# Products of constants on TensorE in the last steps of a decode attention and behind the first piece of its output matrix

## The chip, the cores and the metric

The kernel runs on one core of one Trainium2 chip. The metric is the device time of one execution in microseconds; the time before is the median of three runs. The profile is one further execution, recorded by the hardware profiler.

## The reference

One decode step of a block: a layer norm, attention over a window of a cache with an output matrix, and a gated feed-forward branch whose SiLU multiplies the attention's result.

```python
def _A_ref(x, k_cache, v_cache, wq, wo):
    B, Sq, D = x.shape
    Hq, Dh = 32, 128
    Hkv, Sk = k_cache.shape[1], k_cache.shape[2]
    W = min(4096, max(256, Sk // 4))
    rep = Hq // Hkv
    q = (x @ wq).reshape(B, Sq, Hq, Dh)   # heads to the front
    k = jnp.repeat(k_cache[:, :, Sk - W:, :], rep, axis=1)
    v = jnp.repeat(v_cache[:, :, Sk - W:, :], rep, axis=1)
    scores = jnp.einsum("bhqd,bhkd->bhqk", q, k) * (Dh ** -0.5)
    p = _softmax(scores, axis=-1)
    o = jnp.einsum("bhqk,bhkd->bhqd", p, v)
    return o.reshape(B, Sq, Hq * Dh) @ wo   # heads back in place

def _B_ref(x, w_gate, w_up, w_down):
    return (_gelu(x @ w_gate) * (x @ w_up)) @ w_down

x = A_x
xn = _layernorm(x, axis=-1)
s = _A_ref(xn, A_k_cache, A_v_cache, A_wq, A_wo)
g = _silu(_B_ref(xn, B_w_gate, B_w_up, B_w_down))
return x + s * g
```

There are 8 batch rows, one query position, D = 512, 32 query heads on 8 key heads of width 128, a cache of 4096 positions of which the last 1024 count, and F = 1792. All inputs are bf16. K and V of the window are 16 MiB each, wq and wo 4 MiB each, the feed-forward weights 5.25 MiB: some 47.6 MB are read once.

## The kernel before, in words

**Transfers.** Everything large comes through one queue, SP's, into a pool `big` of nine buffers, in this order: wq, gate and up weights, then K and V of the key heads in turn (with the down weights among them), and last wo. `load_wo` (L125) fetches wo in seven pieces, listed in `pieces` (L639): heads 0 to 3 whole (2 MB), heads 4 and 5 (1 MB), then heads 6 and 7 in halves, and the last half of head 7 in two quarters.

**Sets and steps.** The attention is cut into 16 sets, two for each key head; a set has four batch rows, whose 1024 positions lie on 32 partitions each. The loop at L578 runs 44 steps, t = 0 to 43; two steps belong to a set, and `s, i = divmod(t, 2)`. The order of instructions on every engine is the order in which the program issues them (`manual_schedule`). One set passes through these stages, some steps apart:

- `transpose_quarter` (L439): TensorE turns K into PSUM tiles `kT_ps`, four buffers of a pool; VectorE (L450) and ScalarE (L452) copy them out in turn. The last set is turned in step 31.
- `scores` (L461): products of the queries (in the tile `zeros`) and the turned K; VectorE (L469) adds a mask and finds maxima.
- `maxima` (L480), `exponentials` (L494, ScalarE), `turn` (L504, VectorE).
- `value_half` (L510): the two halves of the value product, eight matmuls each on four groups of 32 columns of the array, into `o_ps`, of which there is one buffer; after the second half ScalarE copies it to `blk` (L522). In step t it treats half (t - 9) % 2 of set (t - 9) // 2, as long as that set exists: sets 12 to 15 in the steps 33 to 40.
- `gather` (L526): for one key head, sums over partitions of two sets' `blk` (L532), a reciprocal (L537), a scaling (L539), a transposition (L550) into `oR` or, for the last two heads, `oL`. The last three gathers stand in steps 33, 37 and 41.

In the steps 33 to 43 there are, on TensorE, only these: a gather and the last `maxima` in step 33, the value halves in steps 33 to 40, gathers in 37 and 41; steps 42 and 43 issue nothing.

**The output matrix.** Behind the loop, `project` (L618) multiplies each piece of wo with `oR` (heads 0 to 5, L621, on four groups of 32 columns, into `s_ps`) or `oL` (heads 6 and 7, L629, into `l_ps`). Behind piece 1 VectorE copies `s_ps` to `s_sb` (L649); behind piece 2 TensorE adds that into `l_ps` (L652). At the end VectorE multiplies with the gate (L657), adds x (L658), and ScalarE's queue stores the result (L659).

`ident` is a 128 x 128 identity in bf16, made near the start. `zeros` is a tile of 1316 columns that is cleared at the start; its first 1024 columns are the queries from then on that they are written (L345, L347).

Of the kernel before, what the change touches and what calls it, by code (L numbers as in the profile page):

```python
# [12 lines left out]
FP32 = mybir.dt.float32  # L13
# [4 lines left out]
def kernel(  # L18
# [13 lines left out]
    nc = tc.nc  # L32
# [11 lines left out]
    P = nc.NUM_PARTITIONS  # L44
# [8 lines left out]
    NS = Hkv * NB  # L53
# [6 lines left out]
    QP = CP // QT  # L60
# [15 lines left out]
    ps_kT = ctx.enter_context(tc.tile_pool(name="ps_kT", bufs=4, space=PSUM))  # L76
# [64 lines left out]
    for k0, cuts in ((0, (1, 1)), (2, (2,))):  # L141
        t = big.tile([P, 2, Hq * Dh], BF16, name="big")
# [10 lines left out]
    ident = lead.tile([P, P], BF16, name="ident")  # L153
# [15 lines left out]
    zeros = rows.tile([P, sum(sizes)], BF16, name="zeros")  # L169
# [136 lines left out]
    for k in range(NDC):  # L306
        w = wq_rows[k]
        for t in range(NT):
            for g in range(NQB):
# [4 lines left out]
                    start=(k == 0), stop=(k == NDC - 1), skip_group_check=True,  # L314
# [39 lines left out]
    for w, src in enumerate((B_w_gate, B_w_up)):  # L354
        for k0 in range(0, NDC, KW):
            wt = load_rows(src, k0, KW, NDC, "gu")
            for k in range(KW):
                for g in range(NQB):
# [3 lines left out]
                        start=(k0 + k == 0), stop=(k0 + k == NDC - 1),  # L362
# [73 lines left out]
    def transpose_quarter(s, i):  # L436
        ps = ps_kT.tile([P, QP, P], FP32, name="kT_ps")
        for c in range(QP):
            nc.tensor.transpose(  # L439
                ps[:, c, :],  # L440
                K[s][:, 2 * (i * QP + c) : 2 * (i * QP + c) + 2, :]
                .rearrange("p c d -> p (c d)").bitcast(FP32),
                identf,
            )
        if i == 0:
            kT[s] = kT_pool.tile([P, CP, P, 2], BF16, name="kT")
        out = kT[s][:, i * QP : (i + 1) * QP].rearrange("p c k e -> p (c k e)")
        in_ = ps.rearrange("p c k -> p (c k)").bitcast(BF16)
        if i % 2 == 0:
            nc.vector.tensor_copy(out=out, in_=in_)  # L450
        else:
            nc.scalar.activation(out=out, in_=in_, func=ACT.Copy)  # L452
# [24 lines left out]
    def maxima(s):  # L477

        ps = m_top
        nc.tensor.matmul(  # L480
            ps, top.pop(s).to_broadcast([P, P]), identf, start=True, stop=True
        )
        scr = small.tile([P, P], FP32, name="scr", bufs=1)
        bias = small.tile([P, 1], FP32, name="bias")
        nc.vector.tensor_tensor_reduce(  # L485
            out=scr, in0=ps, in1=same.rearrange("p x n -> p (x n)"),
            op0=ALU.add, op1=ALU.min, scale=-scale, scalar=-NEG, accum_out=bias,
        )
        biases[s] = bias

    def exponentials(s):
        blk[s] = small.tile([P, 2, Dh + 1], FP32, name="blk", bufs=6)
        P_[s] = p_pool.tile([P, CP * 32], BF16, name="p")
        nc.scalar.activation(  # L494
            out=P_[s], in_=sc.pop(s), func=ACT.Exp, scale=scale, bias=biases.pop(s),
            accum_out=blk[s][:, 0, Dh : Dh + 1],
        )
        nc.gpsimd.tensor_copy(  # L498
            out=blk[s][:, 1, Dh : Dh + 1], in_=blk[s][:, 0, Dh : Dh + 1]
        )  # L500

    def turn(s):
        pT[s] = p_pool.tile([P, CP, 32], BF16, name="pT", bufs=5)
        nc.vector.transpose(  # L504
            out=pT[s].rearrange("p c k -> p (c k)"), in_=P_.pop(s)
        )
# [3 lines left out]
    def value_half(s, i):  # L510
        if i == 0:
            o_ps[s] = ps_o.tile([P, 2, Dh], FP32, name="o_ps")
        for c in range(i * CP // 2, (i + 1) * CP // 2):
            q = c % NR
            nc.tensor.matmul(  # L515
                o_ps[s][32 * q : 32 * q + 32].rearrange("p c d -> p (c d)"),
                pT[s][:, c, :],
                V[s][:, 2 * c : 2 * c + 2, :].rearrange("p c d -> p (c d)"),
                start=(c < NR), stop=(c >= CP - NR), skip_group_check=True,
            )  # L520
        if i == 1:
            nc.scalar.activation(out=blk[s][:, :, 0:Dh], in_=o_ps.pop(s), func=ACT.Copy)  # L522
            pT.pop(s)
            V.pop(s)

    def gather(h):  # L526

        ps = m_out
        for b in range(NB):
            t = blk.pop(h * NB + b)  # L530
            for c in range(2):
                nc.tensor.matmul(  # L532
                    ps, sums[:, c, b].rearrange("p j b f -> p (j b f)"), t[:, c, :],
                    start=(b == 0 and c == 0), stop=(b == NB - 1 and c == 1),
                )
        rec = small.tile([P, 1], FP32, name="rec")
        nc.vector.reciprocal(out=rec, in_=ps[:, Dh : Dh + 1])  # L537
        o = small.tile([P, rep, Dh // rep], BF16, name="o")
        nc.vector.tensor_scalar(  # L539
            out=o, in0=ps[:, 0:Dh].rearrange("p (i r) -> p r i", r=rep),  # L540
            scalar1=rec, scalar2=None, op0=ALU.mult,
        )

        if h < HM:
            out = oR[:, h].rearrange("p r b -> p (r b)")
        else:

            out = oL[:, h - HM].rearrange("p (f y) -> p f y", f=NQB)[:, :, 0:128]
            out = out.rearrange("p f (y z) -> p y f z", z=PB)[:, :, :, 0]
        nc.vector.transpose(out=out, in_=o.rearrange("p r i -> p (r i)"))  # L550


    down_tiles = []
    AHEAD = 3
# [6 lines left out]
    def fetch(kind, h):  # L561
        while True:
            k, i = pending.pop(0)
            if k == "D":
                down_tiles.append(load_rows(B_w_down, 0, NFC, NFC, "wd"))
            else:
                sets = load_pair(
                    A_k_cache if k == "K" else A_v_cache, i,
                    2 if (k, i) in (("V", Hkv - 1),) else 1,
                )  # L570
                for y in range(NB):
                    (K if k == "K" else V)[NB * i + y] = sets[y]
            if (k, i) == (kind, h):
                return
# [3 lines left out]
    for t in range(2 * NS + LV + 3):  # L578
        s, i = divmod(t, 2)
        if i == 0 and 0 <= s - 2 < NS:  # L580
            exponentials(s - 2)
        if s < NS:
            if i == 0 and s % NB == 0:
                fetch("K", s // NB)
            transpose_quarter(s, 2 * i)
        if i == 1 and s >= 6 and s % 2 == 0:
            gather((s - 6) // 2)
        if s < NS:
            transpose_quarter(s, 2 * i + 1)
        for _ in range(2):  # L590
            if hidden_steps:
                hidden_steps.pop(0)()
        if i == 0 and 0 <= s - 2 < NS:
            turn(s - 2)
        if i == 0 and 0 <= s - 1 < NS:
            scores(s - 1)
        if i == 1 and 0 <= s - 1 < NS:
            maxima(s - 1)
        if t == LV - 1:
            fetch("D", 0)  # L600
            down(0)
        if t == LV:
            down(1)
        if t == LV + 1:
            fold()
            gate()
        s3, i3 = divmod(t - LV, 2)
        if 0 <= s3 < NS:
            if i3 == 0 and s3 % NB == 0:
                fetch("V", s3 // NB)  # L610
            value_half(s3, i3)


    s_ps = ps_s.tile([P, 128], FP32, name="s")
# [3 lines left out]
    def project(h, r):  # L618
        for q in range(NQB):
            if h < HM:  # L620
                nc.tensor.matmul(  # L621
                    s_ps[32 * q : 32 * q + 32, :], oR[:, h, r, :],
                    ws[h, r][:, q * 128 : (q + 1) * 128],
                    start=(h == 0 and r == 0), stop=(h == HM - 1 and r == rep - 1),
                    skip_group_check=True,
                )
            else:
                a = q * 128 + r * 32
                nc.tensor.matmul(  # L629
                    l_ps, oL[:, h - HM, a : a + 32],  # L630
                    ws[h, r][:, q * 128 : (q + 1) * 128],
                    start=(h == HM and r == 0 and q == 0),
                    stop=(h == Hkv - 1 and r == rep - 1 and q == NQB - 1),
                    skip_group_check=True,
                )
# [6 lines left out]
    for n, (h0, r0, nr, nh) in enumerate(pieces):  # L642
        t = load_wo(h0, r0, nr, nh)
        for h in range(h0, h0 + nh):
            for r in range(r0, r0 + nr):
                ws[h, r] = t[h - h0][:, r - r0, :]
                project(h, r)
        if n == 1:
            nc.vector.tensor_copy(out=s_sb, in_=s_ps)  # L649
        if n == 2:  # L650

            nc.tensor.matmul(  # L652
                l_ps, pick, s_sb, start=False, stop=False, skip_group_check=True
            )
# [37 lines left out]
```

## Time and profile before

| | |
|---|---|
| median of three runs | 120.62 us (120.59 to 120.70) |
| the profiled execution's own time | 120.43 us |
| its span, first to last instruction | 118.7 us |
| TensorE busy | 83.3 us, 70% of the span, 976 matmuls |
| VectorE, ScalarE, GpSimd busy | 65.1, 56.2, 6.7 us |
| SP's queue | 47.45 MB, 95.3% of 16 engines' span |
| mean rate of the transfers | 401 GB/s |
| chain that ended last | DMA 73%, TensorE 10%, VectorE 8% |

The span runs from the first to the last instruction of the program; the execution's time has 1.7 us around it. A row of the timeline merges instructions that follow each other: start, duration from the first's start to the last's end, engine, line, operation, tiles, shapes, count, and in brackets how long the engine was idle before and who ended that. The ends of matmuls are modelled and overlap with the next ones' starts. In the slices each digit is a fortieth of the span, in tenths of it busy.

### The profile page before, as it was taken

The page shows a single profiled execution, that of the slowest core. Times are in us where ns is not written, and L with a number is a line of the kernel's source. Part 1 is how long each engine was busy: PE and PEld are TensorE (multiplying, and loading weights), DVE is VectorE, ACT ScalarE, POOL GpSimd, SP SyncE. Part 2 cuts the span into 40 slices and gives each one's busy share as a digit, 9 for nine tenths or more (in the row PEclk, how much of TensorE's full clock was granted, in tenths as well). Part 3 has the DMA queues.
Part 4 walks back from the last instruction along what each step waited for, and adds up shares of the span by engine and source line. Part 5 has one row for each costly group of instructions (what it writes and reads, how often), then busy time and mean ns, then how long its engine had stood idle before and what let it go on. Part 6 is the DMA issues. An engine that isn't in the chain of part 4 may idle for free.

```text
span 118.7 us, 2391 instructions
## 1 busy us (share of the span) xinstructions
PE 83.3 (70%) x976; PEld 58.6 (49%) x976; DVE 65.1 (55%) x172; ACT 56.2 (47%) x94; POOL 6.7 (6%) x29
## 2 busy tenths in 40 slices
PE   0070639519956399699999969787795988776390
PEld 0020216119743366377677547555573755555380
DVE  0410131812799899648678658485673955734301
ACT  0500030204961887838685884676565577232000
POOL 7400000000000000000000000000000000000000
PEclk9999999999999999999999999999999999999999
DMA  3999999999999999999999999999999999999950
GB/s 99 425 450 442 401 449 403 431 431 423 423 453 414 423 425 425 428 420 428 428 431 420 425 428 425 420 431 425 425 431 428 420 428 434 413 416 420 410 192 3
DMA packets 6825, 47.60 MB, mean 401 GB/s; under 512 B 536, under 2 KB 800, under 8 KB 1952
## 3 DMA queue, kind: packets, MB, share of 16 engines
q1 hardware_dynamic: 6752, 47.45, 95.3%
q8 instruction: 7, 0.11, 0.3%
q10 hardware_dynamic: 64, 0.02, 0.1%
q14 instruction: 2, 0.02, 0.0%
HBM read 47.46 MB, written 0.01 MB: 400 GB/s over the span
## 4 chain that ended last, share of the span: by engine, by line
DMA 73%; PE 10%; DVE 8%; ACT 3%; SPq 2%; issue 1%
DMA big<-in_A_k_cache_dram 47%; DMA big<-in_A_wo_dram 26%; PE kT_ps L439 6%; PE sc L629 2%; DVE h_row L387 2%; DVE sc_sb L469 1%; DVE pT L504 1%; ACT L380 1%; SPq L145 1%; DVE kT L450 1%; SPq L96 1%; ACT kT L452 1%; PE s L407 1%; ACT p L494 1%; PE sc L461 1%
## 5 line engine op out<-in xcount | busy, mean ns | idle before, releaser
L452 ACT ACTIVATE kT<-kT_ps 128x1024 bf16<-128x1024 bf16 x32 | 32.4, 1020 | 23.4 <-PE kT_ps L439 23.2
L439 PE MATMUL kT_ps<-identf,big 128*128 128x128 f32 x256 | 37.7, 292 | 6.7 <-DMA big<-in_A_k_cache_dram 6.7
L439 PEld LDWEIGHTS kT_ps<-identf,big 128*128 128x128 f32 x256 | 30.1, 149 | 14.2 <-DMA big<-in_A_k_cache_dram 8.5
L450 DVE COPY kT<-kT_ps 128x1024 bf16<-128x1024 bf16 x32 | 22.0, 688 | 15.9 <-PE kT_ps L439 15.6
L494 ACT ACTIVATE p<-sc_sb,bias 128x512 bf16<-128x512 f32 x16 | 11.5, 718 | 6.7 <-DVE bias L485 6.3
L515 PE MATMUL o_ps<-big,pT 128*32 128x256 bf16 x256 | 12.5, 274 | 2.7 <-ACT blk L522 1.5
L504 DVE STREAM_TRANSPOSE pT<-p 128x512 bf16<-128x512 bf16 x16 | 11.3, 705 | 2.6 <-ACT p L494 2.4
L480 PE MATMUL m_ps<-identf,top 128*128 128x128 f32 x32 | 7.3, 310 | 5.9 <-DVE top L469 4.1
L469 DVE CUSTOM_DVE_ANT_0 sc_sb<-sc,own 128x512 f32<-128x512 f32 x16 | 10.5, 654 | 0.0
L461 PE MATMUL sc<-kT,zeros 128*32 128x512 bf16 x128 | 10.0, 388 | 0.5 <-ACT kT L452 0.5
L515 PEld LDWEIGHTS <-pT 128*32 128x32 bf16 x256 | 5.8, 94 | 7.6 <-issue 1.9
L532 PE MATMUL m_ps<-blk,sums 128*128 128x129 f32 x64 | 9.3, 286 | 0.0
L480 PEld LDWEIGHTS m_ps<-identf,top 128*128 128x128 f32 x32 | 4.7, 187 | 8.1 <-DVE top L469 4.9
L532 PEld LDWEIGHTS m_ps<-blk,sums 128*128 128x128 f32 x64 | 8.1, 191 | 0.9 <-issue 0.2
L498 POOL COPY blk<-blk 128x1 f32<-128x1 f32 x16 | 2.9, 183 | 97.3 <-ACT p L494 97.3
L522 ACT ACTIVATE blk<-o_ps 128x256 f32<-128x256 f32 x16 | 6.1, 382 | 3.0 <-PE o_ps L515 3.0
L311 PE MATMUL sc<-big,zeros 128*32 128x512 bf16 x16 | 2.5, 612 | 4.3 <-DMA big<-in_A_wq_dram 3.9
L318 DVE CAST q_row<-sc 128x512 bf16<-128x512 f32 x2 | 1.3, 686 | 7.5 <-PE sc L311 7.5
L485 DVE CUSTOM_DVE_ANT_0 scr<-m_ps,same 128x128 f32<-128x128 f32 x16 | 4.6, 289 | 1.4 <-PE m_ps L480 1.4
L322 ACT ACTIVATE q_row<-o_ps 128x512 bf16<-128x512 f32 x2 | 1.1, 594 | 7.6 <-PE o_ps L311 7.6
L194 PE MATMUL s<-ident,xhat 8*128 8x8 bf16 x4 | 0.3, 174 | 6.2 <-DVE xhat L185 6.2
L311 PEld LDWEIGHTS <-zeros 128*32 128x32 bf16 x32 | 1.1, 120 | 6.4 <-issue 5.8
(77 smaller groups left out, 61.0 us busy)
## 6 DMA issues: line engine op xcount, KB each, us to landing
big<-in_A_k_cache_dram SPq DMA_DIRECT2D x8, 2048.0 KB, 33.0
big<-in_A_v_cache_dram SPq DMA_DIRECT2D x7, 2048.0 KB, 33.7
big<-in_A_wq_dram SPq DMA_DIRECT2D x2, 1024.0 KB, 5.7
big<-in_A_wq_dram SPq DMA_DIRECT2D x1, 2048.0 KB, 11.2
big<-in_A_v_cache_dram SPq DMA_DIRECT2D x2, 1024.0 KB, 28.9
big<-in_A_wo_dram SPq DMA_DIRECT2D x1, 2048.0 KB
big<-in_B_w_gate_dram SPq DMA_DIRECT2D x1, 1792.0 KB, 15.0
big<-in_B_w_up_dram SPq DMA_DIRECT2D x1, 1792.0 KB, 18.5
```

The costliest lines, as they stand in the source:

```text
L439: nc.tensor.transpose(ps[:, c, :], K[s][:, 2 * (i * QP + c) : 2 * (i * QP + c) + 2, :] .rearrange("p c d -> p (c d)").bitcast(FP32), identf,)
L450: nc.vector.tensor_copy(out=out, in_=in_)
L452: nc.scalar.activation(out=out, in_=in_, func=ACT.Copy)
L461: nc.tensor.matmul(ps[32 * R : 32 * R + 32], qT[:, e, s].rearrange("p c b j -> p (c b j)"), t[:, :, 32 * R : 32 * R + 32, e], start=(e == ...
L469: nc.vector.tensor_tensor_reduce(out=sc[s], in0=ps.rearrange("p c k -> p (c k)"), in1=own.rearrange("p c b g -> p (c b g)"), op0=ALU.add, ...
L480: nc.tensor.matmul(ps, top.pop(s).to_broadcast([P, P]), identf, start=True, stop=True)
L485: nc.vector.tensor_tensor_reduce(out=scr, in0=ps, in1=same.rearrange("p x n -> p (x n)"), op0=ALU.add, op1=ALU.min, scale=-scale, scalar=- ...
L494: nc.scalar.activation(out=P_[s], in_=sc.pop(s), func=ACT.Exp, scale=scale, bias=biases.pop(s), accum_out=blk[s][:, 0, Dh : Dh + 1],)
L504: nc.vector.transpose(out=pT[s].rearrange("p c k -> p (c k)"), in_=P_.pop(s))
L515: nc.tensor.matmul(o_ps[s][32 * q : 32 * q + 32].rearrange("p c d -> p (c d)"), pT[s][:, c, :], V[s][:, 2 * c : 2 * c + 2, :].rearrange("p ...
L522: nc.scalar.activation(out=blk[s][:, :, 0:Dh], in_=o_ps.pop(s), func=ACT.Copy)
L532: nc.tensor.matmul(ps, sums[:, c, b].rearrange("p j b f -> p (j b f)"), t[:, c, :], start=(b == 0 and c == 0), stop=(b == NB - 1 and c == 1),)
```

## The change

A helper `keep(n)` is added. It takes a fresh tile of the pool behind `kT_ps` and issues n matmuls into it, with the identity as the stationary operand and the first 512 columns of `zeros` as the moving one. It is called with 2 at the end of each step t of the loop with t > 32, and with 3 behind the matmuls of the first piece of the output matrix. Nothing reads the tiles.

```diff
@@ -548,6 +548,12 @@
         nc.vector.transpose(out=out, in_=o.rearrange("p r i -> p (r i)"))
+
+    def keep(n):
+
+        ps = ps_kT.tile([P, QP * P], FP32, name="kT_ps")
+        for _ in range(n):
+            nc.tensor.matmul(ps, ident, zeros[:, 0 : QP * P], start=True, stop=True)
 
 
     down_tiles = []
@@ -609,6 +615,8 @@
             if i3 == 0 and s3 % NB == 0:
                 fetch("V", s3 // NB)
             value_half(s3, i3)
+        if t > 2 * NS:
+            keep(2)
 
 
     s_ps = ps_s.tile([P, 128], FP32, name="s")
@@ -645,6 +653,8 @@
             for r in range(r0, r0 + nr):
                 ws[h, r] = t[h - h0][:, r - r0, :]
                 project(h, r)
+        if n == 0:
+            keep(3)
         if n == 1:
             nc.vector.tensor_copy(out=s_sb, in_=s_ps)
         if n == 2:
```

Here P is 128, QP is 4 and NS is 16.

## The prediction

> **What bounds the kernel now.** I read the page's slices first, then the end of the chain in order of time, then TensorE's timeline in the last 13 us.
>
> ```profile
> PE   0070639519956399699999969787795988776390
> ...
> DMA  3999999999999999999999999999999999999950
> ```
>
> The transfers run without a break from the first slice to the 38th: the span is what 47.6 MB need at about 425 GB/s, plus what is left to do once the last piece is there. The chain in order of time shows that rest (start, duration, what):
>
> ```profile
> 82.17 30.54 DMA big<-in_A_wo_dram
> 112.70 0.04 issue
> 112.75 0.63 PE s L621 x32
> 113.38 0.00 issue
> 113.38 0.61 PE sc L629 x8
> ```
>
> Until 112.70 the output matrix is being fetched. From 112.75 to 115.79 TensorE multiplies nearly without a gap, and then come two small VectorE steps and the store. So work added on TensorE before 112.75 is free only as far as it fits into TensorE's waits; all beyond that moves the end one for one. The waits are in TensorE's timeline (start, duration, instruction, in brackets the idle time before and who ended it):
>
> ```profile
> 102.98 0.62 PE L515 MATMUL o_ps<-big,pT 128*32 128x256 bf16 x16
> 104.64 0.62 PE L515 MATMUL o_ps<-big,pT 128*32 128x256 bf16 x16 [1.04 <-ACT blk L522]
> 105.19 1.27 PE L532 MATMUL m_ps<-blk,sums 128*128 128x129 f32 x8
> 106.39 0.62 PE L515 MATMUL o_ps<-big,pT 128*32 128x256 bf16 x16
> 107.50 0.62 PE L515 MATMUL o_ps<-big,pT 128*32 128x256 bf16 x16 [0.49 <-ACT blk L522]
> 108.05 1.27 PE L532 MATMUL m_ps<-blk,sums 128*128 128x129 f32 x8
> 110.30 1.08 PE L621 MATMUL s<-big,oR 128*32 128x128 bf16 x64 [0.98 <-DMA big<-in_A_wo_dram]
> 112.75 0.63 PE L621 MATMUL s<-big,oR 128*32 128x128 bf16 x32 [1.37 <-DMA big<-in_A_wo_dram]
> ...
> 114.09 1.69 PE L629 MATMUL sc<-big,oL 128*32 128x128 bf16 x24
> ```
>
> Each row of 16 is the two halves of one value product (L510). Idle is printed from the modelled end of a product, which lies up to 0.2 us behind the moment at which the next could start; I count from start to start.
>
> **The change, part by part.** It removes and moves nothing, issues no transfer, and puts 25 products of 512 columns into TensorE's stream: two at the end of each of the steps t = 33 to 43 (22), three behind piece 0 of the output matrix. Step 33 holds the first half of the value product of set 12, so the first pair stands inside the row at 102.98; pairs follow each of the eight halves up to set 15 (steps 33 to 40), and three pairs the last gather (steps 41 to 43). Nobody reads the results. Operands and buffers are ready: `ident` and `zeros` were written near the start, and the four buffers of `kT_ps` had their last reader at 98.81 + 1.02 = 99.83.
>
> Price of one product: the trace has none of 512 columns on the full 128*128 array. Nearest from above: L333, the same array with bf16, whose rows of 128 columns follow each other at (1.89 - 0.31) / 15 = 0.105 us, so 0.42 for 512. Nearest by length: L461 moves 512 columns through four 32-column groups at once, and its second round starts 0.22 behind the first:
>
> ```profile
> 99.88 0.40 PE L461 MATMUL sc<-kT,zeros 128*32 128x512 bf16 x4 [0.52 <-ACT kT L452]
> ...
> 100.10 0.40 PE L461 MATMUL sc<-kT,zeros 128*32 128x512 bf16 x4
> ```
>
> From below: if products could run four side by side as these do, 0.22 / 4 = 0.055 each. A product on all 128 columns leaves no room beside it, and L629 just behind gives the same pace ((1.69 - 0.22) / 23 = 0.06 for 128 columns with its wait, 0.056 without), so I take **0.22**. 22 of them: 4.84 us.
>
> Price of a change between the 128*32 and the 128*128 array: eight L439 at 95.89 are followed by L461 at 96.91, 1.02 later; four L439 at 92.48 are followed by L532 of their own shape at 92.97, 0.49 later. The four more cost 4 x 0.109 = 0.44, so the change of shape costs 1.02 - 0.49 - 0.44 = 0.09. L515 to L439 (95.56 to 95.89, two rounds of 0.11) gives 0.11; I take 0.095. Before the matrix the pairs add eight changes behind the halves and six back, and take two away (half to gather): 12 x 0.095 = 1.14. The first weights after a change are not loaded ahead: 0.49 - 4 x 0.109 = 0.055, eight times 0.44. The other way, a gather behind a pair finds its own array shape and both results already copied out: at 92.97 such a gather took 1.06 against 1.27 here, so two of them give back 0.42. Sum before the matrix: 4.84 + 1.14 + 0.44 - 0.42 = **6.00 us**.
>
> Three behind piece 0: 3 x 0.22 + 2 x 0.095 + 0.055 = **0.90 us**.
>
> What hides it. First, the two waits for ScalarE's copy L522: sixteen products are four rounds of 0.11, so from 102.98 to 104.64 lie 1.66 - 0.44 = 1.22 idle, and from 106.39 to 107.50 0.67; together 1.89. With a pair behind each half, the copy (0.39) runs under the pair (0.44 + 0.15) and TensorE no longer waits for it; if a copy came later than its pair, the next half would wait as now and no time beyond 1.89 is lost. Second, the wait for piece 0: TensorE is free at 108.05 + 1.20 = 109.25 and starts at 110.30, 1.05. It will now be free at 109.25 + 6.00 - 1.89 = 113.36, so piece 0 starts 3.06 late. Third, the wait for piece 1: 64 products take 16 rounds of 0.055 and the next could start at 111.21, but starts at 112.75, 1.54; 0.90 of products go in, 0.64 is left. Piece 1 then starts at 113.36 + 0.92 + 0.90 = 115.18, **2.43 late**, and from there TensorE waits for no transfer, since all of the matrix has landed by then (the transfers' share is zero from 115 on). That gives back the waits inside the last 3 us: 1.69 - (23 x 0.056 + 0.22) = 0.18 in the last 24 products, and 0.05 of the 0.19 between L621 and L629, because L652 still needs the copy s_sb, which follows L621. Net 2.43 - 0.23 = **2.20 us**. The last gather's VectorE chain (1.38 us from gather to oL) ends near 113.6, ahead of its reader near 117. Whoever waits for the late matmuls is L657, L658 and the store, in line; SP's loads wait for K and V tiles of earlier sets only, so no transfer starts later.
>
> The profiled execution took 120.43 us (118.7 of span and 1.7 around it), 0.19 under the median of 120.62 of the runs shown. 120.43 + 2.20 = 122.63; on the median 122.82. I say **122.8**. Unknown: the product (0.20 to 0.24 is 0.5 either way), the weights' first load (0 or twice as much: 0.5), the gathers' 0.42 given back or not. 122.0 to 123.8.
>
> **Where a rule bears on it.** Row: L333 at 18.80 ran 128 columns in 0.105, L629 at the end in 0.056, twice as fast, though the granted clock reads 1.00 in both windows; so the pace is read from spacing here.
>
> ```profile
> 18.80 1.89 PE L333 MATMUL kT_ps<-ident,q_row 128*128 128x128 bf16 x16
> ```
>
> The Trainium skill, "TensorE: Matmul & The Clock Gate", Part 1, says that the array runs at half rate until activity over a window of about 3.4 us releases it, and falls back after an idle window. By that rule products without use could pay, if they kept the array from falling back. TensorE's longest idle time from 102.98 on is 1.37 us, and the spacing stays at 0.056 to the end: the trace shows nothing to win back.
>
> **The rivals.**
> *Hidden* (not slower): the products run side by side like L461's, 0.055 each. Then 22 x 0.055 + 1.14 + 0.44 - 0.42 = 2.37, less 1.89, is 0.48, inside the 1.05 ahead of piece 0, and the three cost 0.41 inside 1.54: 120.6. It decides below a price of 0.22 - 2.20 / 25 = 0.13 per product. For it: nothing reads them. Against: their weights fill all 128 columns. 5%.
> *Faster array*: in the timed runs, unlike the profiled one, the matmuls of the last 3 us run slow, and the products cure it. The whole excess of the median over the profiled time is 0.19, and a slow tail would cost some 40 steps x 0.05 = 2 us, so at best 120.4, and only if the products were hidden too. 3%.
> *Buffers*: each pair must wait until an earlier write into `kT_ps` has ended (0.40 for one product against 0.22 spacing, 0.18 more for each of 11 pairs): 2.0 more, 124.8. Against: writer and writer are one engine. 6%.
> *Slow pace*: 0.42 per product as in L333: 25 x 0.20 = 5.0 more, 127.8. Against: the pace of all rows near them. 2%.
>
> **How the numbers follow.** The forecast has 84%; its own range of 122.0 to 123.8 leaves out the rivals, 16%. What a measurement here can tell from no change is about 0.2%, 0.24 us. Faster: 3%. Within: 5%. Slower: 92%.
>
> **What would show it.** Right: pairs of about 0.22 spacing behind each half; no wait for L522 between halves; piece 0 starting near 113.4 and piece 1 near 115.2 without a wait for the transfer, the last L629 ending near 118.0, transfers as before. Wrong: piece 0 still released by its transfer (hidden), L629 spacing below 0.055 (faster array), waits ahead of the pairs (buffers), 0.42 apart (slow pace).

## The result and the profile after

| | before | after |
|---|---|---|
| median | 120.62 us (5 runs) | 122.36 us (5 runs) |
| lowest to highest | 120.45 to 121.92 | 122.19 to 122.54 |
| profiled execution, its span | 120.43, 118.7 us | 122.43, 120.7 us |
| busy TensorE | 83.3 us | 89.0 us |

The ratio is 1.0125, with a 95% interval of 1.0083 to 1.0167: slower by 1.74 us, where 2.2 was forecast. The kernel before ran beside the experiments too, 115 times in all counting e0 and the five above: 89 runs lie between 120.44 and 121.04 (median 120.65), 25 between 121.55 and 122.06 (median 121.83), with nothing in between. One at 191.8, and one of e1 at 150.0 (its trace has a granted clock of 0.56 from 32.5 us to the end), belong to neither group.

The slices of the profile after (the page's second part; each digit is a fortieth of the span, in tenths):

```profile
PE   0070738329854599879999999869778796999990
...
PEclk9999999955999769999999999999999999999999
DMA  3999999999999999999999999999999999999800
```

The transfers now end in the 38th slice and TensorE works on to the end of the 39th; before, both ended in the 39th. TensorE's last slices are full. The chain that ended last says the same by engine; before, TensorE had 10% of it:

```profile
DMA 46%; PE 38%; DVE 7%; ACT 3%; issue 2%; SPq 2%
```

TensorE's timeline of the end (start, duration, engine, line; L556 is the added product, L629 and L637 are L621 and L629 of before):

```profile
103.16 0.40 PE L515 MATMUL o_ps<-big,pT 128*32 128x256 bf16 x8
103.49 0.61 PE L556 MATMUL kT_ps<-zeros,ident 128*128 128x512 bf16 x2
104.03 0.40 PE L515 MATMUL o_ps<-big,pT 128*32 128x256 bf16 x8
104.36 0.60 PE L556 MATMUL kT_ps<-zeros,ident 128*128 128x512 bf16 x2
104.92 0.40 PE L515 MATMUL o_ps<-big,pT 128*32 128x256 bf16 x8
...
106.57 1.06 PE L532 MATMUL m_ps<-blk,sums 128*128 128x129 f32 x8
107.55 0.40 PE L515 MATMUL o_ps<-big,pT 128*32 128x256 bf16 x8
...
111.85 1.46 PE L556 MATMUL kT_ps<-zeros,ident 128*128 128x512 bf16 x6
113.24 1.08 PE L629 MATMUL s<-big,oR 128*32 128x128 bf16 x64
114.25 0.82 PE L556 MATMUL kT_ps<-zeros,ident 128*128 128x512 bf16 x3
115.00 0.63 PE L629 MATMUL s<-big,oR 128*32 128x128 bf16 x32
115.46 0.61 PE L637 MATMUL sc<-big,oL 128*32 128x128 bf16 x8
116.03 0.41 PE L662 MATMUL sc<-s_sb,pick 128*32 128x128 f32 x2
116.27 1.50 PE L637 MATMUL sc<-big,oL 128*32 128x128 bf16 x24
```

No row has a bracket any more: the profile shows no idle time of TensorE from 103.16 to the end. (The product at 116.03 still follows VectorE's copy of the sum, which ends at 115.98, as forecast.) Piece 0 starts at 113.24 instead of 110.30, piece 1 at 115.00 instead of 112.75, and the last product ends at 117.77 instead of 115.78.

### The profile page after: what moved, and what is told of

Its sections match the earlier page's. It is cut to its first block, busy times and chain, and to the rows that moved or that the text cites. A ratio compares the mean times of both kernels' runs of the same rounds, so it can differ in the third digit from the quotient of the medians.

```text
span 120.7 us, 2441 instructions
## 1 busy us (share of the span) xinstructions
PE 89.0 (74%) x1001; PEld 60.0 (50%) x1001; DVE 65.2 (54%) x172; ACT 56.2 (47%) x94; POOL 6.7 (6%) x29
## 4 chain that ended last, share of the span: by engine, by line
DMA 46%; PE 38%; DVE 7%; ACT 3%; issue 2%; SPq 2%
DMA big<-in_A_v_cache_dram 26%; DMA big<-in_A_k_cache_dram 19%; PE kT_ps L439 14%; PE kT_ps L556 5%; PE o_ps L515 5%; PE sc L461 4%; PE m_ps L532 3%; PE m_ps L480 2%; DVE h_row L387 2%; ACT kT L452 2%; PE sc L637 1%; PE s L629 1%; ACT L380 1%; SPq L145 1%; DVE sc_sb L469 1%
## 5 line engine op out<-in xcount | busy, mean ns | idle before, releaser
L452 ACT ACTIVATE kT<-kT_ps 128x1024 bf16<-128x1024 bf16 x32 | 32.5, 1021 | 23.6 <-PE kT_ps L439 23.3
L439 PE MATMUL kT_ps<-identf,big 128*128 128x128 f32 x256 | 38.4, 296 | 6.1 <-DMA big<-in_A_k_cache_dram 6.1
L439 PEld LDWEIGHTS kT_ps<-identf,big 128*128 128x128 f32 x256 | 30.8, 151 | 13.5 <-DMA big<-in_A_k_cache_dram 7.3
L515 PE MATMUL o_ps<-big,pT 128*32 128x256 bf16 x256 | 13.2, 275 | 1.2 <-DMA big<-in_A_v_cache_dram 1.2
L515 PEld LDWEIGHTS <-pT 128*32 128x32 bf16 x256 | 5.3, 94 | 8.2 <-issue 2.1
L522 ACT ACTIVATE blk<-o_ps 128x256 f32<-128x256 f32 x16 | 6.1, 383 | 5.2 <-PE o_ps L515 5.2
L556 PE MATMUL kT_ps<-zeros,ident 128*128 128x512 bf16 x25 | 7.1, 383 | 0.0
L537 DVE RECIPROCAL rec<-m_ps 128x1 f32<-128x1 f32 x8 | 1.4, 169 | 6.6 <-PE m_ps L532 6.5
```

What stands on the lines that cost most here:

```text
L439: nc.tensor.transpose(ps[:, c, :], K[s][:, 2 * (i * QP + c) : 2 * (i * QP + c) + 2, :] .rearrange("p c d -> p (c d)").bitcast(FP32), identf,)
L515: nc.tensor.matmul(o_ps[s][32 * q : 32 * q + 32].rearrange("p c d -> p (c d)"), pT[s][:, c, :], V[s][:, 2 * c : 2 * c + 2, :].rearrange("p ...
L556: nc.tensor.matmul(ps, ident, zeros[:, 0 : QP * P], start=True, stop=True)
```

## The experiments

All are compared with the kernel before, run on the same chip. The edits of e1 to e5, e9 and e10 are shown against after, those of e6, e8 and e11 against before, and that of e7 against e6.

**e0: the kernel before again.**

> The kernel before, unchanged. Theory (the 25 products cost what does not fit into TensorE's waits): ratio 1.000, last product of the matrix ending near 115.8. Rival (part of the 1.74 us is the slower array that the profile of after shows from 40.7 to 44 us, where eight L439 took 1.91 instead of 1.04): if that fall comes by chance, it shows in some runs of this kernel too, and its time then moves by up to the 0.17 us by which set 12 began late in after; a granted clock near 0.96 here with a time of 120.6 would say that the fall costs nothing.

Median 120.60 us (12 runs, 120.44 to 121.87, two of them at 121.87), ratio 0.9992 (0.9955 to 1.0029). The granted clock of one run varies between 0.94 and 1.00, and 0.94 occurs at 120.61 as well as at 121.87: a fall need not cost anything, as the rival's second half has it. Its trace has one near the end. TensorE's timeline, and the windows (stretch, length, busy us and count by engine, then granted clock, share and rate of the transfers):

```profile
103.08 0.62 PE L515 MATMUL o_ps<-big,pT 128*32 128x256 bf16 x16
104.74 1.00 PE L515 MATMUL o_ps<-big,pT 128*32 128x256 bf16 x16 [1.04 <-ACT blk L522]
105.67 2.09 PE L532 MATMUL m_ps<-blk,sums 128*128 128x129 f32 x8
107.69 0.87 PE L515 MATMUL o_ps<-big,pT 128*32 128x256 bf16 x16
```

```profile
102.00:104.00 2.00, 1.06 (x19) 0.73 (x19) 1.13 (x5) 0.39 (x1) 0.00 (x0) 1.00 1.00 420
104.00:106.00 2.00, 1.26 (x17) 0.83 (x17) 0.71 (x1) 0.91 (x4) 0.18 (x1) 0.71 1.00 414
106.00:108.00 2.00, 2.00 (x16) 1.72 (x19) 0.17 (x1) 0.17 (x1) 0.00 (x0) 0.50 1.02 422
108.00:110.00 2.00, 1.51 (x35) 1.02 (x28) 1.09 (x2) 0.66 (x2) 0.00 (x0) 0.94 1.02 418
```

Behind the wait for L522 the clock falls to 0.50, the gather takes 2.09 instead of 1.27, and the clock comes back after about 3.4 us (2 x 0.29 / 0.5 + 2 + 2 x 0.06 / 0.5 from the clock column). The last value product starts at 109.06 instead of 107.50, but piece 0 only at 110.81, and it still ends ahead of piece 1's landing: the span stays at 118.8. So the array does fall in the last steps, in some runs, and whether that costs depends on where it falls. The next question was whether the 25 runs at 121.8 are falls inside the output matrix.

**e1, e9: pairs in the loop only.**

```diff
-        if n == 0:
-            keep(3)
```

> Pairs in steps 33 to 43 as in after, none behind piece 0. Theory: the three behind piece 0 took 0.85 us of TensorE (1.76 less 0.91 from the start of piece 0 to that of piece 1) and nothing hides them in after, since piece 1 had landed; without them 0.8 to 0.9 less than after, 121.5. Rival (the three are hidden in the wait for piece 1, all of the loss is in the loop): as after, 122.4.

> e1 once more, for its trace: its median of 121.86 is 0.35 above what the theory made of it. If the theory's terms hold, piece 0 starts 2.8 us later than in the kernel before and piece 1 0.91 behind it, last product 1.0 later than before; else the row with the additional 0.2 to 0.35 us is between the start of piece 0 and the last product.

e1: median 121.86 (12 runs with the one at 150.0; 121.84 without), ratio 1.0085 (1.0053 to 1.0117), 0.5 less than after instead of 0.8 to 0.9. e9 (one run, 122.16) has the trace:

```profile
111.75 1.46 PE L556 MATMUL kT_ps<-zeros,ident 128*128 128x512 bf16 x6
113.14 1.52 PE L629 MATMUL s<-big,oR 128*32 128x128 bf16 x96
114.49 0.61 PE L637 MATMUL sc<-big,oL 128*32 128x128 bf16 x8
...
115.30 1.50 PE L637 MATMUL sc<-big,oL 128*32 128x128 bf16 x24
```

Pieces 0 and 1 follow each other without a gap, and the last product ends at 116.80, 1.02 later than before, 0.97 earlier than in after. Set 12 began at 103.05 here and at 103.16 in after; less that 0.11, the three took 0.86 of the path: the theory's number. The spans of e1's runs (119.7 to 119.9) say the same. The missing 0.35 us lies around the span: 1.9 to 2.7 us there, 1.7 to 1.95 in the kernel before. What takes it was not found. The rival, that the three are hidden in after, falls.

**e2, e10: the three behind piece 0 only.**

```diff
-        if t > 2 * NS:
-            keep(2)
```

> Only the three products behind piece 0. Theory: 0.85 us goes into the 1.54 us in which TensorE waits for piece 1: 120.6, ratio 1.000. Rival (the array slows down in that wait and the products keep it fast): 120.4 or less, with a shorter spacing of L621 or L629 than 0.055. Rival (products delay piece 1 anyhow): 121.4.

> e2 once more, for its share of runs near 121.8: three products behind piece 0 alone. Theory A: none of 12, as in e2, against one in five of the kernel before, median as before. Theory B: two or three of 12.

e2: median 120.63, ratio 0.9978 (0.9949 to 1.0006). e10: 120.58, ratio 0.9967 (0.9937 to 0.9997). TensorE in e2:

```profile
110.63 1.08 PE L627 MATMUL s<-big,oR 128*32 128x128 bf16 x64 [1.02 <-DMA big<-in_A_wo_dram]
111.64 0.82 PE L556 MATMUL kT_ps<-zeros,ident 128*128 128x512 bf16 x3
113.10 0.63 PE L627 MATMUL s<-big,oR 128*32 128x128 bf16 x32 [0.64 <-DMA big<-in_A_wo_dram]
```

The products lie inside the wait, of which 0.64 is left. Of the 24 runs the highest is 120.84; the kernel before had 22% above 121.5.

**e3: one product for two in the steps.**

```diff
-            keep(2)
+            keep(1)
```

> One product in place of two in steps 33 to 43, three behind piece 0. Theory: TensorE gets 11 x 0.216 less, 2.38; piece 0 starts near 111.1, piece 1 near 112.8, at the moment when it lands: 120.6 to 120.8. Rival (the cost is in the changes of the array's shape and the waits around each call, not in the products): those stay, so 121.8 or more.

Median 120.82 (120.69 to 120.98), ratio 0.9991 (0.9963 to 1.0019). As the theory has it, 11 products fewer bring piece 1 back almost to the moment of its landing:

```profile
112.53 0.82 PE L556 MATMUL kT_ps<-zeros,ident 128*128 128x512 bf16 x3
113.28 0.63 PE L629 MATMUL s<-big,oR 128*32 128x128 bf16 x32
```

There is no wait left ahead of it, and the median is 0.17 above that of the lower group of the kernel before. That the calls cost whatever they hold falls.

**e4: the 22 as one block.**

```diff
-        if t > 2 * NS:
-            keep(2)
...
+    keep(22)
```

> The 22 products of the loop as one block behind step 43, three behind piece 0 as in after. Theory (the pairs in the steps are paid in part by the two waits for ScalarE's copy, 1.89 us, and by gathers that are 0.42 shorter): neither is to be had behind the last gather, but 12 changes of the array's shape (1.14) and the first loads go away. Block from 109.15 to 113.90, piece 0 at 114.0, piece 1 at 115.8, last product at 118.5: 123.2 to 123.4, slower than after although it issues the same products. Rival (only the number of products counts): 122.4 as after.

Median 123.58 (123.21 to 124.42, 5 runs), ratio 1.0224 (1.0186 to 1.0263): the same products cost 1.2 us more than in after. Its timeline:

```profile
109.60 4.70 PE L556 MATMUL kT_ps<-zeros,ident 128*128 128x512 bf16 x21
114.22 1.08 PE L629 MATMUL s<-big,oR 128*32 128x128 bf16 x64
...
115.99 0.63 PE L629 MATMUL s<-big,oR 128*32 128x128 bf16 x32
...
117.26 1.50 PE L637 MATMUL sc<-big,oL 128*32 128x128 bf16 x24
```

The last gather began 0.23 later than before in this run; less that, piece 0 is at 113.99, piece 1 at 115.76 and the end at 118.53, as worked out. So the waits for ScalarE's copy did pay for a part of the pairs in after. The profiled execution is the longest of the five, and the array is not the reason: its span ends 3.8 us behind the last product (118.76 to 122.6), in after 2.9 (117.77 to 120.7), with the store in between. What held it up there was not found.

**e5: narrow products.**

```diff
-        for _ in range(n):
-            nc.tensor.matmul(ps, ident, zeros[:, 0 : QP * P], start=True, stop=True)
+        for k in range(n):
+            nc.tensor.matmul(
+                ps[32 * k : 32 * k + 32, :], ident[:, 0:32], zeros[:, 0 : QP * P],
+                start=True, stop=True, skip_group_check=True,
+            )
```

> The same 25 products with 32 weight columns each, the products of one call on neighbouring groups of the array. Theory: no change of shape, and those of one call run side by side, 0.22 for each call instead of 0.53 to 0.65 with its changes: 12 x 0.22 added, of which 1.89 and 1.05 before the matrix and 1.54 behind piece 0 are free: 120.6, and no run near 121.8. Rival (products of one call follow each other whatever their width): 22 x 0.22 = 4.8 before the matrix less 1.89, piece 0 at 112.2, piece 1 at 113.9: 121.5 to 121.8.

Median 120.60 (120.46 to 120.76, 11 runs), ratio 0.9984 (0.9961 to 1.0006). Two of them now run beside each other, and the waits for L522 are back:

```profile
103.12 0.40 PE L515 MATMUL o_ps<-big,pT 128*32 128x256 bf16 x8
103.35 0.38 PE L556 MATMUL kT_ps<-zeros,ident 128*32 128x512 bf16 x2
103.36 0.59 PE L515 MATMUL o_ps<-big,pT 128*32 128x256 bf16 x8
103.78 0.38 PE L556 MATMUL kT_ps<-zeros,ident 128*32 128x512 bf16 x2
104.78 0.40 PE L515 MATMUL o_ps<-big,pT 128*32 128x256 bf16 x8 [0.61 <-ACT blk L522]
```

Piece 1 is waited for again too (0.75 in the timeline). The same 25 products cost nothing when they are 32 columns wide: from 103.35 to 103.78 a pair and a half take 0.43 together, where a half alone takes 0.22, so a product is about 0.11. The narrow ones also change the array's shape nowhere behind a half; how much of the gain is due to that, this run doesn't separate.

**e6, e8: piece 0 left out of the sum.** The runs near 121.8: if they are falls of the array, less work on TensorE must make them more frequent.

```diff
-                    start=(h == 0 and r == 0), stop=(h == HM - 1 and r == rep - 1),
+                    start=(h == 4 and r == 0), stop=(h == HM - 1 and r == rep - 1),
...
-                project(h, r)
+                if n > 0:
+                    project(h, r)
```

> The kernel before with the 64 products of piece 0 (heads 0 to 3 of the output matrix) left out of the sum. Theory A (the runs of the kernel before near 121.8 are those in which the array falls to half rate during the output matrix, after a stretch with little work on TensorE): TensorE now has nothing from 109.25 to 112.75, so the array falls in nearly every run and L621, L629 run at 0.105 to 0.11 per 128 columns instead of 0.055: median 121.6 to 122.4, slower than the kernel before with 64 products fewer. Theory B (the runs near 121.8 come from something else, a transfer for instance, and the tail waits for transfers only): 120.6 median, with the same share near 121.8 as before.

> e6 once more (heads 0 to 3 left out of the sum), for its trace: 8 of 12 of its runs were above 121.5 and the profile fell on one of the others. If this run is above 121.5, theory A: granted clock 0.5 in the windows from 112 us on, eight L629 taking 0.107 each from start to start instead of 0.056, transfers landing as before. Theory B: a late transfer ahead of L621 or L629 and full rate. If it is near 120.6: full rate in the tail, and a fall at another place or none.

e6: median 121.77, ratio 1.0051 (1.0017 to 1.0085): eight of 12 runs at 121.52 or above, with 64 matmuls fewer. e8 was to bring the trace of one; it ran in 120.77 with full rate in the tail, and a fall near 104.9 as in e0. So no run of this kernel near 121.8 has a trace.

**e7: constants in the place of piece 0** (heads 0 to 3 left out here too).

```diff
+        if n == 0:
+            keep(12)
```

> The same (heads 0 to 3 left out of the sum), with 12 products of constants of 512 columns in the place of the 64 products, 2.6 us of work that nobody reads. Theory A: they keep the array at full rate: 120.6, no run near 121.8, L629 at 0.056. Theory B: 120.6 with some runs near 121.8.

Median 120.70 (120.44 to 120.92, 12 runs), ratio 0.9988 (0.9967 to 1.0008), none near 121.8. Work that nobody reads undoes what leaving out the other did, as theory A has it.

**e11: a long idle stretch.** Heads 0 to 5 and the last gather left out.

```diff
-        if i == 1 and s >= 6 and s % 2 == 0:
+        if i == 1 and 6 <= s < 20 and s % 2 == 0:
...
-                project(h, r)
-        if n == 1:
-            nc.vector.tensor_copy(out=s_sb, in_=s_ps)
...
+                if n > 1:
+                    project(h, r)
```

> Left out of the sum: heads 0 to 5 of the output matrix with the copy of their sum, and the last gather (head 7 counts as zero). TensorE then has nothing from 107.9 to 113.4, longer than the 3.4 us for which a fall lasts in every trace so far, and 32 matmuls L629 remain. Theory A (after a stretch with little work the array runs at half rate, and a run near 121.8 is one in which that meets the output matrix): every run is slow there, the trace shows L629 at 0.107 from start to start and a granted clock of 0.5 in the windows from 112 to 116 us; 32 x 0.05 = 1.6 more, partly under the wait for the last pieces: 121.2 to 122.2, slower than the kernel before with 100 matmuls and a gather less. Theory B (the tail waits for transfers only): 120.6 or less, L629 at 0.056.

Median 121.77 (121.43 to 121.98, 12 runs, all above 121.4), ratio 1.0064 (1.0032 to 1.0095). TensorE's end, and the windows:

```profile
107.60 0.62 PE L515 MATMUL o_ps<-big,pT 128*32 128x256 bf16 x16 [0.49 <-ACT blk L522]
113.47 3.31 PE L629 MATMUL sc<-big,oL 128*32 128x128 bf16 x32 [5.25 <-DMA big<-in_A_wo_dram]
```

```profile
108.00:110.00 2.00, 0.22 (x9) 0.09 (x1) 0.01 (x1) 0.39 (x1) 0.00 (x0) 0.88 1.03 422
110.00:112.00 2.00, 0.00 (x0) 0.00 (x0) 0.00 (x0) 0.00 (x0) 0.00 (x0) 0.50 1.01 409
112.00:114.00 2.00, 0.53 (x6) 0.53 (x6) 0.00 (x0) 0.00 (x0) 0.00 (x0) 0.50 0.93 352
114.00:116.00 2.00, 2.00 (x22) 2.00 (x20) 0.00 (x0) 0.00 (x0) 0.00 (x0) 0.50 0.25 89
116.00:118.00 2.00, 0.78 (x10) 0.60 (x8) 0.56 (x2) 0.00 (x0) 0.00 (x0) 0.91 0.00 0
```

32 matmuls take 3.31 us, 0.10 each, where before they and the copy of the sum took 2.4; the clock is at 0.50 from 110 to past 116. The transfers end by 115.5, before by 115.0, while the last product ends at 116.78, 1.0 later than before and at half rate; theory B falls for this kernel. No execution of the kernel before in its upper group was caught with a full trace. That those are falls inside the output matrix is argued from e6, e7 and e11, and from their spans, 119.8 to 120.2 against 118.7 to 119.2: the time is lost inside the program. A late store, as in e4's profile, would lengthen the span as well, but the clocks speak against it: the 24 runs of the upper group with a clock on record all read 0.927 to 0.943, and of the 85 in the lower group 14 read that low. Each run of the upper group thus holds more time at half rate than most others. In e6 three of the eight long runs read 0.986, as the trace of e2 does with a single fall of 3.4 us.

## Why the prediction was right, and where it was off

**The mechanism held term by term.** One product took (1.46 - 0.38) / 5 = 0.216, forecast 0.22 (0.38 is the group's mean of one). A gather behind a pair gives back 0.22 (106.57 to 107.55 against 105.19 to 106.39), forecast 0.21. No half waits for L522, so the 1.89 were used up, as e4 shows from the other side. From piece 0 to piece 1 it was 1.76, forecast 1.82; from piece 1 to the last product's end 2.77, forecast 2.80.

**The terms that were off** are small. Set 12 began 0.18 later in the profile of after than in that of before; less that, the last product ends 1.81 later, where 2.20 was forecast. Most of the missing 0.39 is the first load of weights behind a change of shape, 0.055 taken from an fp32 group: from a half to its pair it was 0.33 (103.49 less 103.16), of which the half takes 0.22, so change and load together are 0.11 where 0.15 was counted, 0.3 less over the eight pairs. The change back was 0.11 (103.49 to 104.03 less two products) instead of 0.095, 0.1 more. The products at 0.216 make 0.09 less, the three behind piece 0 and the tail another 0.09. The forecast had named the first load as unknown, from nothing to twice as much. The medians are 1.74 apart.

**The step that failed,** without harm to the forecast, is the dismissal of the rival "faster array": "The whole excess of the median over the profiled time is 0.19". The three runs shown happened to lie in the lower group. 25 of 114 runs of the kernel before are 1.2 us higher, and none of the 64 runs is that with constants behind piece 0 and the whole sum kept (after 5, e2 12, e3 12, e5 11, e10 12) or in its place (e7 12), each against its own lower end. (e4 has one, 1.2 above its lowest, which is the profiled one with the late end.) So the products do have a benefit; if they take away the whole upper group, it is 25/114 x 1.18 = 0.26 us on average. It takes the three of e2 to have it, which cost nothing; the 22 of the loop cost about what was forecast and pushed even the three onto the path. The rival's condition was wrong as well: not all products need to be hidden, three ahead of piece 1 suffice.

**What the rule said and what the runs show.** I read from "TensorE: Matmul & The Clock Gate" in the Trainium skill, Part 1, that the array falls back after an idle window of about 3.4 us, took it that less idle time does nothing, and set 1.37 us against it. The trace of e0 does not bear that out: it fell behind an idle time of 1.04, in a stretch with some work. The duration agrees: about 3.4 us at 0.50 in e0. The runs' granted clocks agree too: they cluster at 1.00, 0.986, 0.971, 0.957 and 0.942 of 118.8 us, steps of 0.0145 x 118.8 = 1.7 us, half of 3.4: each step is one more fall at half rate.

**The other rivals.** *Hidden* has its condition right: e5 puts the price per product at 0.11, below the break-even of 0.13, and the time is 120.60; but its products need no change of shape behind the halves either. *Buffers* and *slow pace* don't occur: pairs follow the halves at once, 0.216 apart.

**A version ahead of after, and on average of before,** is e2: median 120.60 and mean 120.62 over its 24 runs, against 120.69 and 120.90 over 114 of the kernel before. e10's ratio leaves 1 out of its interval only just, e2's holds it. Against after it saves 1.8 us.

## What to carry to other kernels

Work without use on an in-order engine is free only in the waits behind which nothing is late yet: count the free time up to the last transfer, from start to start, and put filler into the one wait that stands ahead of the end, not into every step. A median of three doesn't show a group of runs that one execution in five belongs to; look at single times and spans before calling an effect impossible. Leaving work out can make a kernel slower, and is a cheap test of that.

## What the runs showed of the hardware

Whether the clock falls behind the same wait differs from run to run. All the kernels issue the same instructions up to step 32, and TensorE waits 2.8 us for maxima just ahead of 40.4 in before and after alike; in ten of the thirteen traces other than e1's a fall begins between 40 and 43 us, and those of before, e7 and e9 have none on record. Three fall near 105 (e0, e6 and e8). Within a trace the falls begin a whole number of 3.41 us apart: 23.7 and 40.7 in after (5 times), 40.0 and 104.8 in e0 (19 times), 41.3 and 109.5 in e11 (20 times), and each lasts 3.4 us or, as the first of after and the last of e11, 6.8. So it looks as if a run had a grid of its own, and a wait made the clock fall only where it meets the grid; that is an inference from these traces.

In after, the fall at 40.7 (windows of TensorE's busy time, clock in the third column from the right) made eight transposes take 1.91 instead of 1.04 and put the stages 1.3 us behind, and yet set 12 came only 0.18 later, since the later stages wait for transfers anyway. Even the 0.18 need not be the fall's: set 12 began between 102.98 and 103.34 in these traces, and at 103.18 in e7, whose clock reads 1.00 throughout.

```profile
40.00:42.00 2.00, 1.58 (x8) 1.58 (x9) 1.42 (x6) 1.53 (x3) 0.00 (x0) 0.68 1.02 433
42.00:44.00 2.00, 2.00 (x14) 0.83 (x13) 1.47 (x3) 1.16 (x3) 0.18 (x1) 0.50 1.01 422
```

Around the span lie 1.7 to 1.95 us in the runs of the kernel before, but 1.9 to 2.7 in e1 and e9. Nothing in the traces names the cause.
